# A planned attention and feed-forward kernel: VectorE chains in the planner, z in contiguous rows, other idle matmuls, a new search of priorities

## The chip, the cores and the metric

One core of a Trainium2 chip. The metric is the device time of one execution in microseconds. In a profile, PE is TensorE's matmuls and PEld its weight loads, DVE is VectorE, ACT is ScalarE, POOL is GpSimd, and SP issues the transfers.

## What is computed

```python
# per batch (8) and head (8), 576 positions, head size 64, 128 features
h   = x_scaled @ omega.T - sum(x_scaled**2) / 2
phi = exp(h - max(h)) / sqrt(128)              # for q and for k
kv  = phi_k.T @ v;  z = sum over positions of phi_k
attn = (phi_q @ kv) / (phi_q @ z + 1e-6)
# then over 4608 tokens of 512 values (heads side by side)
out = softplus(attn @ w_in) @ w_out            # 512 -> 2048 -> 512
```

All arrays are float32. The two layers are done in split form: a rounded part and a rest of both operands, three matmuls of the rounded type for one product.

## The kernel before

**Staging.** Attention is cut in sixteen quads, `Quad(n)`: one batch and four heads each. A quad's 576 positions are five tiles (`NU`), four of 128 positions and one of 64. For each tile of k or q: a load; `squares` and `norms` (sum of squares); for batches 2 to 7 `rounded` and `rest` (the operand split, L497 and L501); `project` on TensorE (L390 in batches 0 and 1, L508 later); `aside` and `join`, which add the two halves of the split projection (L511, L515); `maxima`, `bias`, `exponent` (L518, L525, L526, L530). Key tiles go on to `outer` in `plan_sums` (L589, L591): kv accumulates over tiles 0 to 2 in one bank, is put aside by `part`, and over tiles 3 and 4 in another; then `z` and `whole` add the two. z goes out to memory and comes back to all partitions (L610, L614) as `zb`. Query tiles go on to `den` (L712, four products with accumulation), `invert` (L717), `divide` (L721), `blocks` (a transpose, L744), out and in again by transfers (L757, L767), and to `num` (L834), whose result is split in `xh` and `xl` (L841, L845), the ring of 1024 tokens that layer 1 reads. Batch 0 takes a shorter way: kv in one bank, z spread by a matmul (L669), features turned by TensorE (L728).

**Feed-forward.** Tokens come in four blocks of 256 and seven of 512; each block has 16 steps, one for each 128 of the 2048 inner values. A step is layer 1 (twelve matmuls, L884 to L886, into one of two `h` banks), three activations on ScalarE (L890, L893, L896), `plus` on VectorE (L899, which frees the h bank), `high` and `low` (L903, L907: the split `gh`, `gl`), and layer 2 (three matmuls for each 128 tokens, L913 to L915).

**What sets the order.** Each of these is a `Work` with a cost on one or two engines, a due time, what it comes after, and the buffers that it takes and gives. `in_order` builds one list greedily: of all works that may start, the one that starts first, and of those that could start within PATIENCE of it on the same engine, the one due first. With two engines given (`squares`, `rest`, `divide`, `high`, `low` and others) it takes the one that ends sooner. `LAG` is the time between engines, LATE a margin on some works, and `port` keeps works of VectorE marked so apart from GpSimd's. Instructions are issued in this order, engine by engine, and each engine keeps it. `with_fill` puts idle matmuls, 512 columns each, where the plan has TensorE waiting in its first 70 us. The PSUM banks are two `at` (attention), two `h` and four `acc`; `ph` tiles have six buffers, and a query tile takes two of them (`phs` for the features, `rest` for the products) from `project` on.

Of the kernel before, what the change touches and what calls it, by code (L numbers as in the profile page):

```python
# [41 lines left out]
LEAN = {"DVE": 0.81, "POOL": 0.50, "ACT": 0.19}  # L42
SPREAD = ((0, 24.76), (18, 70.75))
# [6 lines left out]
def blocks_of(n_tokens):  # L50
# [10 lines left out]
    ("POOL", "DVE"): 0.075, ("POOL", "PE"): 0.05, ("ACT", "ACT"): 0.13, ("POOL", "POOL"): 0.1,  # L61
}


class Work:

    def __init__(
        self, on, due, emit, after=(), take=(), give=(), spare={}, behind=None, port=False, late=0.0, wire=None
    ):
        self.on, self.due, self.emit, self.port = on, due, emit, port  # L70
# [3 lines left out]
        self.wire, self.done = wire, None  # L74

# [5 lines left out]
def in_order(works, room, ahead, margin):  # L81
# [35 lines left out]
    while len(out) < len(works):  # L117
# [11 lines left out]
        for n, (_, box, key) in zip(got, w.take):  # L129
# [23 lines left out]
def with_fill(out, held, banks, until, emit):  # L153

    last, all_ = None, []
    for i, w in enumerate(out):
        if w.engine == "PE":
            t = w.end - w.on["PE"] * (2 if w.end < SLOW + 1 else 1)
            n = int((t - last - FILL) / 0.2268) if last is not None and t < until else 0
            names = [  # L160
                b for b in banks if all(x1 <= last and g < i or x0 >= t and f >= i for x0, x1, f, g in held.get(b, []))
            ] if n > 0 else []
            if names:
                all_.append((emit, names[0], n))
# [6 lines left out]
def favor_softplus_kernel(ctx, tc, q0, k0, qx, qy, kx, ky, vv, om, wi, wo, out):  # L171
# [89 lines left out]
    def plan_weights(nm, fc, due):  # L261
# [34 lines left out]
        def low_part(e):  # L296
# [5 lines left out]
            "SP", dma(0.65, 1.22, 1.7), due + 0.01, load, spare={} if last else {"w": 2},  # L302
# [5 lines left out]
        a = do(("ACT", "DVE"), (aw, dw2), due, low_bits, after=[l], port=True)  # L308
        b = do("ACT", aw, due, rebias, after=[l])
        c = do("DVE", dw, due, joined, after=[a, b], port=True)  # L310
        d = do(
            ("ACT", "DVE"), (aw, dw), due, high_part, after=[c] + (in_w if last else []), take=[("w", box, "w")], port=True,
# [17 lines left out]

    def phs(b, kind, n):
        return [("ph", b, (k, i)) for i in range(n) for k in (["phs", "rest"] if kind == "q" else ["phs"])]

    def plan_unit(q, kind, us, due, early):
# [83 lines left out]
        def exponent(j):  # L418
# [12 lines left out]
            "SP", read(size), due - 6.92, load, behind=prev.get("load"),  # L431
# [3 lines left out]
        if kind == "k" and not early:  # L435
            for i in range(len(us)):
                ldv.append(do(
                    "SP", dma(0.7, 1.0, 0.7), due + 3.31, lambda i=i: load_v(i), behind=ld, take=[("v", b, ("vs", i))]
                ))
        s = do(("POOL", "ACT"), (pool(w), act(w)), due, squares, after=[ld])  # L440
        r, sm = None, [("sm", b, "sms")]
        if not cols:
            r = do("DVE", dve(w), due + 1.34, norms, after=[s], behind=prev.get("norms"), take=sm)
# [3 lines left out]
            "PE", 0.29 + (0.44 if cols else 0.224) * nt, due + 0.86, project, after=[ld] + ([s] if cols else []),  # L447
            behind=(prev.get("project"), q.zc if kind == "q" and not early else None),
            take=[(kind_, b, ("ppb", 0)), (kind_, b, ("ppb", 1))] + (sm if cols else []) + ([] if early else phs(b, kind, len(us))),
# [16 lines left out]
        for i in range(len(us)):  # L466
            plan_queries(q, us[i], due - 0.00 * i, b, es, f"{nm}_{i}", i, i == len(us) - 1)

    def plan_split(q, kind, u, due):
# [40 lines left out]
        def aside(t):  # L510
            nc.scalar.copy(b["ph"][:, 2 * t : 2 * t + 2], b["pp"][t][:, :, 1])  # L511
# [16 lines left out]
        def exponent(t):  # L528
# [604 lines left out]
```

## Time and profile before

| | |
|---|---|
| three runs | 1073.42, 1076.78, 1080.35 us, median 1076.78 |
| the profiled execution | 1077.06 us, span 1075.3 us |
| mean granted clock of TensorE | 0.972 |
| largest groups on TensorE | layer 1 at L884 254.2 us, L885 249.2, L886 249.2; layer 2 at L913 230.0, L914 226.0, L915 225.3 |
| projections L508 for k and q | 38.4 and 36.6 us |
| kv at L589 | 41.0 and 14.3 us |
| idle matmuls | 8 of `idle` 3.7 us, 17 of `ident` 4.8 us |

The largest groups on TensorE overlap, since matmuls are pipelined; how closely they follow is read from the starts of single instructions. A row of stretches gives busy time by engine in a range; the clock in it is what TensorE was granted, 1.00 being full.

### The profile page before, as it was taken

To read this page: it belongs to the slowest core of one execution; us is meant where nothing else is said; L and a number is where in the kernel's file an instruction comes from. 1 tells how busy PE (TensorE), PEld (TensorE's weight loads), DVE (VectorE), ACT (ScalarE), POOL (GpSimd) and SP (SyncE) were. 2 spreads that over 40 slices of the span, in tenths; PEclk is the share of its full clock that TensorE was granted. 3 is DMA by queue.
4 is the path that set the end of the run, shared out by engine and by line. 5 is a ranking of instruction groups with operands and counts; after the bars stand their busy time and mean duration, and the time that the engine had idled before them with its cause. 6 is when DMAs were issued, how large, how long until landed. Compare 5 with 4: busy or idle time off the path is not lost.

```text
span 1075.3 us, 17753 instructions
## 1 busy us (share of the span) xinstructions
PE 1034.8 (96%) x5585; PEld 857.5 (80%) x5585; DVE 806.5 (75%) x2342; ACT 746.2 (69%) x1904; POOL 223.1 (21%) x218
## 2 busy tenths in 40 slices
PE   8889999999999999999999999999999999999997
PEld 7777788889887877778777787788778887888886
DVE  7889968888889898989878998888898923223222
ACT  6899967787778777767777676777667644445443
POOL 2032222133324221232232222252201200000000
PEclk7779999999999999999999999999999999999999
DMA  9843226545445454545354535553464302001001
GB/s 345 338 138 99 79 76 176 147 122 138 138 128 158 113 134 122 165 112 142 103 142 140 141 89 142 156 155 99 114 166 117 79 5 79 1 1 40 1 1 39
DMA packets 117902, 125.81 MB, mean 117 GB/s; under 512 B 17840, under 2 KB 92720, under 8 KB 117808
## 3 DMA queue, kind: packets, MB, share of 16 engines
q1 hardware_dynamic: 117808, 124.68, 40.7%
q8 instruction: 44, 0.72, 0.3%
q14 instruction: 50, 0.41, 0.1%
HBM read 98.66 MB, written 25.98 MB: 116 GB/s over the span
## 4 chain that ended last, share of the span: by engine, by line
PE 58%; DVE 26%; ACT 7%; issue 4%; DMA 4%; POOL 0%; SPq 0%; DVEq 0%; ACTq 0%; POOLq 0%
PE h L884 8%; PE h L886 8%; PE h L885 8%; PE acc L913 8%; PE acc L914 7%; PE acc L915 7%; DVE restq L712 5%; PE kv_True L589 3%; DVE u L899 2%; DMA xq<-qy 2%; DVE phk L515 2%; PE xp L834 2%; DVE smk L518 2%; DVE phq L721 2%; DVE phq L515 1%
## 5 line engine op out<-in xcount | busy, mean ns | idle before, releaser
L884 PE MATMUL h<-xh,wi 128*128 128x512 f32 (+1 forms) x704 | 254.2, 361 | 10.7 <-DVE u L899 8.9
L885 PE MATMUL h<-xl,wi 128*128 128x512 f32 (+1 forms) x704 | 249.2, 354 | 0.0
L886 PE MATMUL h<-xh,wi 128*128 128x512 f32 (+1 forms) x704 | 249.2, 354 | 0.0
L913 PE MATMUL acc<-wo,gh 128*128 128x512 f32 x576 | 230.0, 399 | 1.3 <-ACT o L949 1.3
L914 PE MATMUL acc<-wo,gh 128*128 128x512 f32 x576 | 226.0, 392 | 0.0
L915 PE MATMUL acc<-wo,gl 128*128 128x512 f32 x576 | 225.3, 391 | 0.0
L899 DVE SCALAR_TENSOR_TENSOR u<-h,u 128x512 f32<-128x512 f32 (+1 forms) x176 | 102.7, 586 | 132.1 <-ACT u L896 131.3
L884 PEld LDWEIGHTS h<-xh,wi 128*128 128x128 f32 x704 | 134.7, 191 | 36.9 <-DVE u L899 14.6
L890 ACT ACTIVATE u<-h 128x512 f32<-128x512 f32 (+1 forms) x176 | 90.9, 519 | 104.4 <-PE h L886 101.6
L886 PEld LDWEIGHTS h<-xh,wi 128*128 128x128 f32 x704 | 134.7, 191 | 18.3
L885 PEld LDWEIGHTS h<-xl,wi 128*128 128x128 f32 x704 | 134.7, 191 | 17.0
L903 ACT CAST gh<-u 128x512 fp32r<-128x512 f32 (+1 forms) x162 | 87.3, 541 | 73.5 <-PE acc L915 25.2
L907 POOL TENSOR_TENSOR gl<-u,gh 128x256 fp32r<-128x256 f32 (+1 forms) x80 | 86.1, 1078 | 248.7 <-ACT gh L903 237.6
L913 PEld LDWEIGHTS acc<-wo,gh 128*128 128x128 f32 x576 | 108.7, 189 | 26.3 <-issue 5.8
L915 PEld LDWEIGHTS acc<-wo,gl 128*128 128x128 f32 x576 | 108.5, 188 | 23.7
L914 PEld LDWEIGHTS acc<-wo,gh 128*128 128x128 f32 x576 | 108.9, 189 | 17.5
L712 DVE CUSTOM_DVE_ANT_0 restq<-phq,zb 128x128 f32<-128x128 f32 x280 | 113.0, 449 | 8.0 <-ACT phq L530 5.6
L896 ACT ACTIVATE u<-u 128x512 f32<-128x512 f32 (+1 forms) x176 | 97.7, 558 | 3.6
L893 ACT ACTIVATE u<-u 128x512 f32<-128x512 f32 (+1 forms) x176 | 97.7, 558 | 3.2
L501 POOL TENSOR_TENSOR tq<-xq,tq 64x512 fp32r<-64x512 f32 (+1 forms) x47 | 56.2, 1195 | 181.0 <-ACT tq L497 131.7
L530 ACT ACTIVATE phk<-phk,smk 128x128 f32<-128x128 f32 x216 | 70.3, 392 | 29.5 <-DVE smk L526 29.4
L907 DVE TENSOR_TENSOR gl<-u,gh 128x512 fp32r<-128x512 f32 (+1 forms) x96 | 61.3, 639 | 36.6 <-ACT gh L903 33.5
(126 smaller groups left out, 1542.1 us busy)
## 6 DMA issues: line engine op xcount, KB each, us to landing
xk<-ky SPq DMA_DIRECT2D x48, 384.0 KB, 3.5
xq<-qy SPq DMA_DIRECT2D x48, 384.0 KB, 3.3
qdq<-restq SPq DMA_DIRECT2D x56, 256.0 KB, 2.4
out<-o SPq DMA_DIRECT2D x36, 256.0 KB, 2.3
vk<-vv SPq DMA_DIRECT2D x70, 130.0 KB, 3.3
rawi<-wi SPq DMA_DIRECT2D x16, 512.0 KB, 7.2
rawo<-wo SPq DMA_DIRECT2D x16, 512.0 KB, 6.0
q<-qdq SPq DMA_DIRECT2D x64, 128.0 KB, 3.6
```

The source lines that it names most:

```text
L712: nc.vector.tensor_tensor_reduce(jk[r, c], ph[r, c], q.zb[r, h], 1.0, 1e-6, ALU.mult, ALU.add, dn[r, 0, c : c + 1])
L884: nc.tensor.matmul(b["h"], wh, xh[:, cc, t], start=cc == 0, stop=False)
L885: nc.tensor.matmul(b["h"], wh, xl[:, cc, t], start=False, stop=False)
L886: nc.tensor.matmul(b["h"], wl, xh[:, cc, t], start=False, stop=cc == NCC - 1)
L890: nc.scalar.activation(b["u"], b["h"], AF.Abs)
L893: nc.scalar.activation(b["u"], b["u"], AF.Exp, scale=-1.0)
L896: nc.scalar.activation(b["u"], b["u"], AF.Ln, bias=1.0)
L899: nc.vector.scalar_tensor_tensor(b["u"], b["h"], 0.0, b["u"], ALU.max, ALU.add)
L907: (nc.vector if e == "DVE" else nc.gpsimd).tensor_tensor(b["gl"], b["u"], b["gh"].bitcast(F32), ALU.subtract)
L913: nc.tensor.matmul(acc[tt], gh, w2[fc][:, 0], start=fc == 0, stop=False)
L914: nc.tensor.matmul(acc[tt], gh, w2[fc][:, 1], start=False, stop=False)
L915: nc.tensor.matmul(acc[tt], gl, w2[fc][:, 0], start=False, stop=fc == NFC - 1)
```

## The change

- **Planner.** `lag` between two dependent works on VectorE is 0.11 us instead of 0. A work has `soon` (it may start that much before one of its inputs is done), `steps` (stored, not used) and `heat` (columns that it streams); a taken buffer may be needed later than the start (a fourth entry in `take`). Costs of several works are set anew: `den` 0.87 for 1.27, a kv tile 0.836 for 0.89; `blocks` is marked as using the shared port.
- **Buffers.** `ph` is no longer taken at `project` but at `aside` or the first `exponent`, and `rest` at `den`.
- **kv.** One work for each key tile instead of one for all; the first may start before the last tiles are done.
- **z.** In memory [4, 128] instead of [128, 4], so that `zb` lies with the features side by side.
- **Idle matmuls.** The first eight become four each of 512, 256, 128 and 64 columns. Later ones go wherever the plan has a gap that holds one and a free bank, while fewer than 2.95 x 8192 columns were streamed in the last 3.41 us; the old rule now leaves 5.58 us of a gap (before 0.3).
- **Numbers.** All due times, LATE, PATIENCE, LEAN, SPREAD, AHEAD are searched anew.

The diff, cut to its core:

```diff
-AHEAD = 52.88
+AHEAD = 213.44
-LATE = {"num": 1.83, "turn": 3.02, "project": 0.72, "blocks": 0.00, "out": 0.00, "in": 0.07, "store": 0.10, "outer": 0.52}
+LATE = {"num": 1.25, "turn": 5.44, "project": 0.85, "blocks": 0.00, "out": 0.27, "in": 2.55, "store": 0.24, "outer": 0.27}
-SLOW = 6.63
-FILL = 0.3
-PATIENCE = {"PE": 0.00, "DVE": 0.02, "ACT": 0.00, "POOL": 0.02, "SP": 0.19}
+SLOW = 7.59
+FILL = 5.58
+UNTIL = 93.76
+HEAT = 2.95
+EXTRA = 0.00
+WINDOW = 3.4133
+PATIENCE = {"PE": 0.00, "DVE": 0.01, "ACT": 0.00, "POOL": 1.23, "SP": 1.02}
...
+    ("DVE", "DVE"): 0.11,
...
-            data = max([x.done + lag(x.engine, e) for x in w.after], default=0.0)
-            space = max([free[n][0] + lag(free[n][1], e) for n in got], default=0.0)
+            data = max([x.done + lag(x.engine, e) - w.soon.get(x, 0) for x in w.after], default=0.0)
+            space = max([free[n][0] + lag(free[n][1], e) - sum(k[3:]) for n, k in zip(got, w.take)], default=0.0)
...
-            n = int((t - last - FILL) / 0.2268) if last is not None and t < until else 0
...
+                n = int((t - last - FILL) / 0.2268) if t < UNTIL else 0
+                cool = HEAT * 8192 - sum(h for s, h in hot if s > t - WINDOW)
+                n = max(n, min(int(np.ceil(cool / 512)), int((t - last) / 0.2268 + EXTRA)))
...
-            take=[(kind_, b, ("ppb", 0)), (kind_, b, ("ppb", 1))] + (sm if cols else []) + ([] if early else phs(b, kind, len(us))),
+            take=[(kind_, b, ("ppb", 0)), (kind_, b, ("ppb", 1), 0.1 * nt)] + (sm if cols else []), heat=512 * nt,
...
-            q.zd = dram.tile([P, 4], F32, name=f"zd{q.nm}", tag="zd", bufs=2)
-            nc.sync.dma_start(q.zd, q.z)
+            q.zd = dram.tile([4, P], F32, name=f"zd{q.nm}", tag="zd", bufs=2)
+            nc.sync.dma_start(q.zd.rearrange("c m -> m c"), q.z)
...
-            "PE", 0.03 + sum(0.89 if u < 4 else 0.45 for _, _, u in keys), due + 0.10, outer, after=deps,
+    for k, (b, i, u) in enumerate(keys):
+        m = do(
+            "PE", 0.836 if u < 4 else 0.418, due + 0.62, lambda k=k: outer(k), after=[m] if k else [x for x, _ in deps],
+            soon={} if k else dict(deps), take=[] if k else [("at" if q.b > 1 else "more", y, "bank")],
...
-            "DVE", 1.27, due - 0.54, den, after=es + [q.zc], take=[("dn", b, "dns")],
+            "DVE", 0.87, due - 2.57, den, after=es + [q.zc], steps=4, soon={es[1]: 0.43} if q.b > 1 and u < 4 else {},
...
-        fill("at.0", 8, idle)
+        for i in range(4):
+            fill("at.0", 4, idle[:, : P if i < 3 else D], max(1, 4 >> i))
```

How the rows stand, at three places. First, TensorE at the start (`fill` are idle matmuls, `ppk_1_1` the projection of the second key tile of quad 1, `kv_0` quad 0's kv). Before, and then in the change:

```order
L390 MATMUL ppk_1_1_0_178<-omf,xk_1_1_110 128x128
L390 MATMUL ppk_1_1_1_179<-omf,xk_1_1_110 128x128
L390 MATMUL ppk_0_2_0_194<-omf,xk_0_2_112 128x128
L390 MATMUL ppk_0_2_1_195<-omf,xk_0_2_112 128x128
L390 MATMUL ppk_0_2_0_194<-omf,xk_0_2_112 128x128
L390 MATMUL ppk_0_2_1_195<-omf,xk_0_2_112 128x128
L645 MATMUL kv_0_220<-xk_0_0_104 128x65 x4
L645 MATMUL kv_0_220<-xk_0_1_108 128x65 x4
```

```order
L400 MATMUL ppk_1_1_0_198<-omf,xk_1_1_125 128x128
L400 MATMUL ppk_1_1_1_199<-omf,xk_1_1_125 128x128
L1043 MATMUL fill<-ident 128x512 x3
L400 MATMUL ppk_0_2_0_226<-omf,xk_0_2_127 128x128
L400 MATMUL ppk_0_2_1_227<-omf,xk_0_2_127 128x128
L400 MATMUL ppk_0_2_0_226<-omf,xk_0_2_127 128x128
L400 MATMUL ppk_0_2_1_227<-omf,xk_0_2_127 128x128
L662 MATMUL kv_0_242<-xk_0_0_117 128x65 x4
L1043 MATMUL fill<-ident 128x512 x2
```

Three idle matmuls now stand ahead of a projection and two behind the first kv; from the first projection to the turning of the first query tile there are 25 of 512 columns, where before there were five, and in the whole kernel 33 behind the initial ones instead of 17.

Second, GpSimd in the last batch (`tq_0_0` is the rest of the first query tile of that batch, `gl` a step's rest, `phq` a division). Before, and then in the change:

```order
L501 TENSOR_TENSOR tq_1_4_9326<-xq_1_4_9263,tq_1_4_9326 64x256
L907 TENSOR_TENSOR gl_11_9364<-u_11_9274,gh_11_9330 128x512
L501 TENSOR_TENSOR tk_1_0_9384<-xk_1_0_9311,tk_1_0_9384 64x512
L501 TENSOR_TENSOR tq_0_0_9442<-xq_0_0_9390,tq_0_0_9442 64x512
L721 TENSOR_TENSOR phq_1_4_9370<-phq_1_4_9370,dnq_1_4_9434 128x256
L501 TENSOR_TENSOR tk_1_1_9503<-xk_1_1_9424,tk_1_1_9503 64x512
L501 TENSOR_TENSOR tq_0_1_9557<-xq_0_1_9474,tq_0_1_9557 64x512
L907 TENSOR_TENSOR gl_15_9662<-u_15_9594,gh_15_9654 128x512
```

```order
L512 TENSOR_TENSOR tk_0_4_9269<-xk_0_4_9161,tk_0_4_9269 64x256
L925 TENSOR_TENSOR gl_9_9285<-u_9_9232,gh_9_9274 128x512
L738 TENSOR_TENSOR phq_1_3_9260<-phq_1_3_9260,dnq_1_3_9321 128x512
L738 TENSOR_TENSOR phq_1_4_9391<-phq_1_4_9391,dnq_1_4_9431 128x256
L925 TENSOR_TENSOR gl_14_9640<-u_14_9590,gh_14_9634 128x512
```

`tk_1_0`, `tq_0_0`, `tk_1_1` and `tq_0_1` are no longer on GpSimd; they stand on VectorE. Over the whole kernel GpSimd has 12 `gl` of 512 columns instead of 39, 6 whole `tq` instead of 36, 11 `tk` instead of 20, 2 weight parts instead of 9, but 30 whole divisions instead of 17 and 14 half ones instead of 4. Of the roundings ScalarE has 91 whole ones instead of 57, and VectorE 5 instead of 39; of the `high` casts of 512 columns ScalarE has 110 instead of 101.

Third, kv on TensorE (`vk_1_0`, `vk_1_1`, `vk_1_2` are the v of the first three key tiles of a quad). Before, and then in the change:

```order
L915 MATMUL acc_1_2680<-wo_1376,gl_10_3179 128x512
L589 MATMUL kv_1_2_True<-vk_1_0_2811,phk_1_0_2827 128x65 x4
L589 MATMUL kv_1_2_True<-vk_1_1_2824,phk_1_1_2986 128x65 x4
L589 MATMUL kv_1_2_True<-vk_1_2_2984,phk_1_2_3118 128x65 x4
L884 MATMUL h_14_3287<-xh,wi_1449 128x256
```

```order
L933 MATMUL acc_1_2790<-wo_1446,gl_9_3204 128x512
L606 MATMUL kv_1_2_True<-vk_1_0_2687,phk_1_0_2842 128x65 x4
L606 MATMUL kv_1_2_True<-vk_1_1_2849,phk_1_1_3036 128x65 x4
L606 MATMUL kv_1_2_True<-vk_1_2_3008,phk_1_2_3172 128x65 x4
L902 MATMUL h_13_3288<-xh,wi_1428 128x256
```

The three tiles follow each other in both. From batch 1 on there are 28 such runs of key tiles before and 29 in the change, so only one is parted.

More of the change, by code (lines that the diff above doesn't have):

```diff
@@ L315, in plan_weights @@
             in_w.append(d)
-        return do(("DVE", "POOL"), (dw, pw), due, low_part, after=[d], give=[(box, "raw")], port=True)
+        return do(("DVE", "POOL"), (dw, pw), due - 6.73, low_part, after=[d], give=[(box, "raw")], port=True)
     class Quad:
@@ L615, in in_z @@
-            q.zb = t.rearrange("p m c -> p c m")
+            q.zb = at.tile([P, 4, M], F32, name=f"zb{q.nm}", tag=q.slots["zb"], bufs=1)
+            nc.sync.dma_start(
+                q.zb.rearrange("p c m -> p (c m)"), q.zd.rearrange("c m -> (c m)").unsqueeze(0).broadcast_to([P, 4 * M])
+            )
         old = quads[q.n - 3].nums if q.n >= 3 else []
-        m = do(
-            "PE", 0.03 + sum(0.89 if u < 4 else 0.45 for _, _, u in keys), due + 0.10, outer, after=deps,
-            take=[("at" if q.b > 1 else "more", y, "bank")],
-            give=[(b, (k, i)) for b, i, _ in keys for k in ("phs", "vs")],
-            late=LATE["outer"] if q.b > 1 else 0, behind=() if first else tuple(old),
-        )
+        m = None
@@ L624, in plan_sums @@
+        for k, (b, i, u) in enumerate(keys):
+            m = do(
+                "PE", 0.836 if u < 4 else 0.418, due + 0.62, lambda k=k: outer(k), after=[m] if k else [x for x, _ in deps],
+                soon={} if k else dict(deps), take=[] if k else [("at" if q.b > 1 else "more", y, "bank")],
+                give=[(b, ("phs", i)), (b, ("vs", i))], heat=1040,
+                late=LATE["outer"] if q.b > 1 and not k else 0, behind=None if k or first else tuple(old),
+            )
         if first:
-            q.part = do("ACT", 0.29, due - 0.33, part, after=[m] + ([quads[q.n - 1].kvl] if q.n > 2 else []), give=[(y, "bank")])
+            q.part = do("ACT", 0.29, due - 25.64, part, after=[m] + ([quads[q.n - 1].kvl] if q.n > 2 else []), give=[(y, "bank")])
@@ L805, in plan_queries @@
         h = do(
-            ("ACT", "DVE"), (act(n * M, PSUM), dve(n * M)), due + 3.71, turned, after=[t], give=[(b, "tpb")],
+            ("ACT", "DVE"), (act(n * M, PSUM), dve(n * M)), due + 19.16, turned, after=[t], give=[(b, "tpb")],
         )
@@ L847, in plan_x @@
         a = do(
-            "PE", 0.26 + 0.00334 * w, due - 8.94, num, after=q.turned + [q.kvl],
-            take=[(any_, y, ("bank", p)) for p in range(2)], give=[(qt, k) for k in (["tag"] if not q.b else [("tag", i) for i in range(nq)])],
+            "PE", 0.16 + 0.00334 * w, due + 2.89, num, after=q.turned + [q.kvl], heat=8 * w,
+            take=[(any_, y, ("bank", p), (0.08 + 0.00167 * w) * p) for p in range(2)], give=[(qt, k) for k in (["tag"] if not q.b else [("tag", i) for i in range(nq)])],
             behind=tuple(old_reads(q.b, o, w)),
@@ L952, in store @@
                 nc.sync.dma_start(out[t0 + tt * P : t0 + (tt + 1) * P, :], o["t"])
-            a = do("DVE", 0.34, due + 1.55, left, after=[ends[tt]], take=[("t2", o, "s")])
-            r = do("ACT", 0.27, due - 1.98, right, after=[a], give=[(box, ("acc", i, tt))])
-            do("SP", dma(0.25, 0.8, 1.05), due + 8.00, store, after=[a, r], give=[(o, "s")], late=LATE["store"])
+            a = do("DVE", 0.34, due - 9.45, left, after=[ends[tt]], take=[("t2", o, "s")])
+            r = do("ACT", 0.27, due - 18.81, right, after=[a], give=[(box, ("acc", i, tt))])
+            do("SP", dma(0.25, 0.8, 1.05), due - 20.96, store, after=[a, r], give=[(o, "s")], late=LATE["store"])
     assert NQ == 2
```

202 lines of the change are left out of this document (105 added, 97 removed).

## Prediction

> **What bounds the kernel now.** I read the page first, then the stretches, then what TensorE waits for, then single instructions.
>
> The head of the page, and the shares of the chain that ended last:
>
> ```profile
> span 1075.3 us, 17753 instructions
> PE 1034.8 (96%) x5585; PEld 857.5 (80%) x5585; DVE 806.5 (75%) x2342; ACT 746.2 (69%) x1904; POOL 223.1 (21%) x218
> ...
> PE 58%; DVE 26%; ACT 7%; issue 4%; DMA 4%; POOL 0%; SPq 0%; DVEq 0%; ACTq 0%; POOLq 0%
> ```
>
> TensorE is the bound, and VectorE stands on the chain for a quarter of it. The profiled execution took 1077.06 us, 0.03% over the median of the three runs (1076.78), so 1.8 us lie around its span; I subtract from 1077.06. Three stretches (after the range: length, then PE, PEld, DVE, ACT and POOL busy, clock, DMA share, GB/s):
>
> ```profile
> 0.00:80.00 80.00, 69.20 (x410) 57.78 (x411) 63.20 (x264) 64.07 (x168) 17.44 (x27) 0.74 0.74 276
> 80.00:860.00 780.00, 755.96 (x4235) 627.88 (x4234) 684.30 (x1987) 584.24 (x1572) 205.70 (x192) 0.99 0.47 127
> 860.00:1075.30 215.30, 209.66 (x944) 171.81 (x942) 58.97 (x92) 97.85 (x166) 0.00 (x0) 1.00 0.07 21
> ```
>
> The last stretch is the feed-forward alone and has nothing to give: it is idle for 5.6 us in all, most of it behind the last matmul. The middle has 24.0 us of idle TensorE, with VectorE busy 88% of it (684.30 of 780). The start runs at 0.74 of the clock. The granted clock falls to half in seven stretches; two long and one short of them:
>
> ```profile
> 11.80:35.70 23.90, 23.90 (x127) 22.29 (x126) 18.07 (x69) 17.34 (x51) 4.41 (x8) 0.50 1.03 391
> 49.30:66.40 17.10, 14.16 (x61) 10.82 (x62) 15.99 (x69) 14.32 (x33) 2.88 (x3) 0.50 0.49 157
> ...
> 769.50:772.90 3.40, 3.40 (x9) 2.65 (x9) 3.19 (x7) 2.87 (x9) 0.78 (x1) 0.50 0.62 152
> ```
>
> The other four (at 134.7, 407.7, 465.7 and 520.4 us) are as short as the last. What TensorE and its weight loads wait for (us in total, times, longest):
>
> ```profile
> PEld h L884 <- DVE u L899: 14.6, 18, 2.7
> PEld kv_True L589 <- DVE phq L515: 6.7, 8, 1.5
> PEld ppq L508 <- POOL tq L501: 5.8, 4, 2.8
> ```
>
> Layer 1 waits for VectorE's `plus` to free an h bank, kv waits for a `join` to free a bank, and a query projection waits for GpSimd. One such wait in full, on TensorE and then on GpSimd (start, length, engine, line, what):
>
> ```profile
> 768.74 0.74 PE L508 MATMUL ppq<-oms,tq 128*128 128x256 f32 x4 [2.37 <-POOL tq L501]
> ...
> 770.39 0.63 PE L884 MATMUL h<-xh,wi 128*128 128x512 f32 x1
> 770.82 0.63 PE L885 MATMUL h<-xl,wi 128*128 128x512 f32 x1
> ...
> 773.42 0.39 PE L886 MATMUL h<-xh,wi 128*128 128x512 f32 x1
> 773.65 0.39 PE L913 MATMUL acc<-wo,gh 128*128 128x512 f32 x1
> ```
>
> ```profile
> 767.42 1.26 POOL L501 TENSOR_TENSOR tq<-xq,tq 64x512 fp32r<-64x512 f32 x1 [6.46 <-ACT tq L497]
> ```
>
> TensorE stands 2.37 us for a 1.26 us subtraction on GpSimd, and right behind it comes a half-clock stretch in which a 512-column matmul starts 0.43 us after the one before it, against 0.23 us at full clock. So a wait is paid twice: 2.37 us, and then half of 3.40 us.
>
> **z contiguous.** Before, the four values of a feature lie side by side, so the products at L712 step over `zb` by 16 bytes. The tiles of batch 0 read a contiguous `zb` (copied from PSUM); all others read the strided one:
>
> ```profile
> 58.60 0.29 DVE L712 CUSTOM_DVE_ANT_0 xq<-xq,zb 128x128 f32<-128x128 f32 x1
> ...
> 58.82 0.28 DVE L712 CUSTOM_DVE_ANT_0 xq<-xq,zb 128x128 f32<-128x128 f32 x1
> ```
>
> ```profile
> 568.15 0.38 DVE L712 CUSTOM_DVE_ANT_0 restq<-phq,zb 128x128 f32<-128x128 f32 x1
> ...
> 568.47 0.38 DVE L712 CUSTOM_DVE_ANT_0 restq<-phq,zb 128x128 f32<-128x128 f32 x1
> ```
>
> ```profile
> L712 DVE CUSTOM_DVE_ANT_0 restq<-phq,zb x280: 369/386/1507, 131.5 to 855.0; 128x128 f32<-128x128 f32 x112, 64x128 f32<-64x128 f32 x28
> ```
>
> From start to start 0.32 us strided, 0.22 us contiguous: 0.10 us for each of 280, **28 us less on VectorE**, all of it in the middle. The price is paid by the write of z, which becomes 512 runs of 4 bytes instead of 128 of 16:
>
> ```profile
> zd<-z SPq DMA_DIRECT2D x14, 2.0 KB, 1.9
> ...
> zb<-zd SPq DMA_DIRECT2D x14, 256.0 KB, 4.3
> ```
>
> Bounds for one: unchanged (1.9 us), or four times it (7.6). Two of the fourteen places, the read of `zb` on SP and the first product on VectorE:
>
> ```profile
> 222.95 0.33 SPq L614 DMA_DIRECT2D zb<-zd  x1
> ```
>
> ```profile
> 226.78 0.39 DVE L712 CUSTOM_DVE_ANT_0 restq<-phq,zb 128x128 f32<-128x128 f32 x1
> ```
>
> ```profile
> 542.57 0.33 SPq L614 DMA_DIRECT2D zb<-zd  x1
> ```
>
> ```profile
> 554.57 0.94 DVE L712 CUSTOM_DVE_ANT_0 restq<-phq,zb 128x128 f32<-128x128 f32 x1
> ```
>
> The first has no room, the second 12.0 - 4.3 = 7.7 us. Behind the waiting read on SP stand the loads of the next tiles and the features' DMAs; in the order of the change other DMAs go between write and read in ten of the fourteen places (before: in nine). A write 5.7 us later would at worst hold the first product for 14 x 5.7 = 80 us; with some 7 us of room at most places I take 0. The Trainium skill's page "DMA: Bandwidth & Descriptors" (Specifications) says that a transfer under 512 B is done as a read-modify-write; by that rule the dearer end is the likelier. No run here shows either end yet.
>
> **Planner, shared port, new priorities.** The order shows who takes what. The rows that price it:
>
> ```profile
> L712 DVE CUSTOM_DVE_ANT_0 restq<-phq,zb 128x128 f32<-128x128 f32 x224 | 89.5, 456 | 6.4 <-ACT phq L530 5.6 <-ACT phq L427 0.3
> ...
> L907 DVE TENSOR_TENSOR gl<-u,gh 128x512 fp32r<-128x512 f32 x73 | 50.5, 691 | 32.7 <-ACT gh L903 29.9 <-PE h L886 0.7
> ...
> L721 DVE TENSOR_TENSOR phq<-phq,dnq 128x512 f32<-128x512 f32 x39 | 33.6, 861 | 1.0
> ...
> L497 DVE CAST tk<-xk 128x512 fp32r<-128x512 f32 x24 | 10.1, 422 | 5.5 <-PE ppq L508 3.2 <-issue 1.1 <-POOL xk L489 0.9
> ...
> L501 DVE TENSOR_TENSOR tq<-xq,tq 64x512 fp32r<-64x512 f32 x12 | 8.3, 690 | 0.4
> ```
>
> ```profile
> L907 POOL TENSOR_TENSOR gl<-u,gh 128x512 fp32r<-128x512 f32 x39 | 52.6, 1348 | 141.1 <-ACT gh L903 132.5 <-issue 4.5 <-DVE gh L903 3.0
> L501 POOL TENSOR_TENSOR tq<-xq,tq 64x512 fp32r<-64x512 f32 x36 | 47.8, 1327 | 136.6 <-ACT tq L497 95.4 <-DVE tq L497 20.6 <-DMA q<-qdq 7.0
> ...
> L721 POOL TENSOR_TENSOR phq<-phq,dnq 128x512 f32<-128x512 f32 x17 | 18.2, 1072 | 11.1 <-DVE dnq L717 10.9
> ```
>
> ```profile
> L497 ACT CAST tk<-xk 128x512 fp32r<-128x512 f32 x24 | 15.0, 623 | 0.5 <-DMA xk<-ky 0.5
> ```
>
> From GpSimd to VectorE: 27 `gl` of 512 columns (27 x 0.691 = 18.7 us on VectorE, 36.4 off GpSimd), 30 `tq` differences (20.7 and 39.8), 9 `tk` (6.2 and 11.9), 7 weight parts (about 4.8 and 9.4). From VectorE to GpSimd: 13 divisions (9.0 at an undisturbed 0.69, 13.9 on GpSimd) and 10 half ones (about 4 and 6). From VectorE to ScalarE: 34 roundings (34 x 0.422 = 14.3, 21.2 on ScalarE) and 9 `gh` (3.8 and 5.6). VectorE gains about 19 us of work, ScalarE 27, and GpSimd loses 78 of its 223, a third.
>
> GpSimd's third matters for the port. While GpSimd works, some of VectorE's instructions stand: the strided products have a median of 386 ns and a maximum of 1507; the divisions have a mean of 861 where the same form of `gl` has 691, 39 x 0.17 = 6.6 us. For the 224 whole products the mean of their group (456) is 70 ns over the median, 15.7 us. A third of these 22 us gone is 7 us. So VectorE's load moves by -28 + 19 - 7 = **-16 us**, 2.3% of 684.
>
> What this is worth on TensorE: VectorE's idle time in the middle grows from 96 to 112 us, and if waits shrink as that grows, the 21.3 us of the first two wait rows (14.6 + 6.7) become 18.3: **-3**. What a better order does to the remaining 18.3 lies between nothing and all of it; the plan now counts 0.11 us between dependent VectorE instructions and a `den` of 0.87 us instead of 1.27, and takes the `ph` buffers later, so I take half: **-9**. It could be worth less than nothing: the margin LATE for `outer` falls from 0.52 to 0.27 and for `num` from 1.83 to 1.25, which puts TensorE's in-order work closer to its data; I bound that by +9. Queued behind such a matmul is all of layer 1, and ScalarE waits for that.
>
> The 5.8 us behind GpSimd: 30 of 36 whole `tq` differences leave it, and the one of the example is among them: 5.8 x 30/36, **-5** (between 0 and -5.8).
>
> **kv one work per tile.** The order keeps the tiles of a run next to each other in all but one of 28 runs, so nothing moves on TensorE: 0. The buffers of the first tiles come free one or two tiles earlier on paper; the bound is the 6.7 us of the kv row, counted above already.
>
> **Idle matmuls.** The five short stretches of half clock cost 5 x 3.40 / 2 = 8.5 us, and the one shown comes right behind a wait. With 17 of the 27 us of the named waits gone about three of the five go: **-5** (between 0 and -8.5); only 8 of the new idle matmuls lie past the early part, so they do not do it themselves. In the early part 25 stand between the first projections and kv. If they hold the clock up, the 23.90 us of work of 11.8 to 35.7 would take 12, but VectorE has 18.07 us of work there and the transfers run at 391 GB/s with a share of 1.03, so at most 5.4 us come free; in 49.3 to 66.4 VectorE's 15.99 leaves 1.1. Bounds 0 and -6.5, **-4** taken, as the clock may rise late in it. The initial eight become sixteen shorter ones, with 3840 columns for 4096: 0.
>
> **Sum.** -3 - 9 - 5 - 5 - 4 = -26: 1077.06 - 26 = **1051 us**.
>
> **Rivals.** *Nearly all waits go.* All 21.3 and 5.8, the dips' 8.5 and 6.5 of the start are 42 us: 1035; with the small waits that the rows don't name a few less, 1030. For it: the tail shows full-rate TensorE when nothing disturbs it. Against: VectorE is still at 86%.
>
> *No relief.* The 19 us moved onto VectorE and 27 onto ScalarE lengthen the chain that layer 1 waits for (ScalarE's three activations, then `plus`), and the 14.6 us row stays. Then only the start and a wait or two give: 1077 - 5 = 1072. For it: ScalarE, not only VectorE, feeds `plus`. Against: its 584 of 780 leave room.
>
> *The idle matmuls stand in the way* (slower). In 11.8 to 35.7 TensorE is busy for 23.90 of 23.90 us and yet at half clock: being busy did not raise it. If 25 matmuls of 512 columns more don't either, each costs 0.43 us on an engine without a gap there, 10.8 us, and with the +9 of thinner margins: 1077 + 20 = 1097. It decides from the point where the gaps that the plan sees (TensorE at full speed after 7.59 us) are not on the chip. The rule cannot hold back: it asks for 2.95 x 8192 = 24166 columns in 3.41 us, and a matmul every 0.23 us gives 7600, so every planned gap is filled. The Trainium skill's page "TensorE: Matmul & The Clock Gate" (Part 1) says that about 3.4 us of sustained work release the full clock; by that rule alone the stretch would have been fast from about 15 us on. The trace disagrees: seven such windows stayed at 0.50. So what counts must be more than busy, which is why I hold the dense idle matmuls for likelier to help than not.
>
> **How the numbers follow.** Forecast (1037 to 1066) 0.60; nearly all waits go 0.12; no relief 0.17; idle matmuls in the way 0.11. Over 1% either way is about what a measurement of this kernel tells from no change: faster 0.72, within 1% 0.17, slower 0.11. The range 1030 to 1075 holds the first three but for their ends. The forecast's own range is 1037 to 1066.
>
> **What would show it.** Right: products at L712's place start 0.21 to 0.22 us apart; GpSimd near 145 us, VectorE near 790, ScalarE near 773; at most two or three short half-clock stretches past 100 us; no wait of `ppq` for GpSimd over 1 us; the half-clock stretch before 36 us shorter. Wrong: TensorE idle for 24 us or more from 80 to 860; clock 0.50 from 12 to 36 with fills in it; VectorE waiting for the landing of `zb`.

## The result and the profile after

The changed kernel takes 1132.23 us (median of 4 runs, 1125.63 to 1133.14) and the kernel before 1075.1 beside it: 1.0514 times as long, 95% interval 1.0453 to 1.0576. The forecast was 1051, 0.976 times, with a range to 1075. It is slower by 57 us where 26 us less were expected. The profiled execution of the change took 1131.58 us. One execution of all that follow is left out of its ratio: of the ten of the write that is called "64 apart" in a table below, one took 2007.92 us (the median in the table is that of all ten).

The page of the changed kernel: span, busy time by engine, and the clock in 40 slices.

```profile
span 1129.8 us, 17905 instructions
PE 1044.1 (92%) x5609; PEld 867.4 (77%) x5609; DVE 752.5 (67%) x2345; ACT 762.1 (67%) x1946; POOL 147.9 (13%) x173
...
PEclk9899898999998989899989999989989899999999
```

GpSimd (147.9) and ScalarE (762.1) are near the 145 and 773 forecast, and VectorE (752.5) is 37 us below the 790. The work has moved as planned, the engines have less of it, and the kernel is slower all the same: all engines stand more. The products, at their new line:

```profile
L729 DVE CUSTOM_DVE_ANT_0 restq<-phq,zb x280: 259/287/1372, 134.6 to 903.3; 128x128 f32<-128x128 f32 x112, 64x128 f32<-64x128 f32 x28
```

The median is 287 ns against 386: the 0.10 us of each product are there. Three stretches of the changed kernel (length, then PE, PEld, DVE, ACT and POOL busy, clock, DMA share, GB/s):

```profile
15.90:50.10 34.20, 31.32 (x251) 25.11 (x248) 27.28 (x130) 30.96 (x88) 2.84 (x4) 1.00 1.01 382
80.00:860.00 780.00, 720.16 (x3995) 604.11 (x3996) 594.42 (x1849) 565.83 (x1530) 133.45 (x150) 0.96 0.48 120
860.00:915.00 55.00, 49.03 (x219) 40.54 (x218) 37.21 (x130) 31.94 (x76) 6.34 (x7) 0.94 0.42 78
```

The start runs at full clock, so the new idle matmuls do not stand in the way. The middle, which now reaches to 915 us, has 780 - 720.16 + 55 - 49.03 = 65.8 us of idle TensorE against 24.0, and a clock of 0.96 and 0.94. Read in rows of 0.8 us, the profile has thirteen half-clock stretches past 100 us, of 3.4 or 6.8 us each, 75 us in all, against five of 3.40 us before, 17 in all. What TensorE waits for (us in total, times, longest):

```profile
PE ppq L518 <- DVE phk L527: 20.1, 7, 4.3
PE ppk L518 <- DVE tk L512: 10.9, 2, 5.8
...
PE ppk L518 <- POOL tk L512: 7.0, 1, 7.0
...
PE h L902 <- DVE u L917: 4.6, 3, 4.1
```

The row of layer 1 has shrunk from 14.6 to 4.6, as was meant. In its place stand few and long waits of the projections, 3 to 7 us each. The engines that they name are not the cause; that is read from the transfers. The waits of SP's queue, first in the changed kernel and then in the kernel before:

```profile
SPq L628 <- DMA zd<-z: 93.0, 13, 9.8
```

```profile
SPq L614 <- DMA zd<-z: 17.0, 10, 2.9
```

And the landing of the two z transfers in the changed kernel (KB each, median us from issue to landing):

```profile
zb<-zd SPq DMA_DIRECT2D x14, 256.0 KB, 5.2
zd<-z SPq DMA_DIRECT2D x14, 2.0 KB, 9.9
```

The write of z lands in 9.9 us where it took 1.9: 5.2 times as long for the same 2 KB, above the dearer bound of 7.6. One of the fourteen places in full (start, length, engine, line, what, and idle time before it):

```profile
554.89 0.38 SPq L624 DMA_DIRECT2D zd<-z  x1
...
556.19 0.35 SPq L489 DMA_DIRECT2D xk<-ky  x1
...
564.92 0.33 SPq L628 DMA_DIRECT2D zb<-zd  x1
...
568.90 0.42 ACT L498 ACTIVATE xk<-xk 128x256 f32<-128x256 f32 x1 [7.80 <-DMA xk<-ky]
...
570.23 1.28 POOL L512 TENSOR_TENSOR tk<-xk,tk 64x512 fp32r<-64x512 f32 x1 [10.01 <-ACT tk L508]
...
571.57 1.22 PE L518 MATMUL ppk<-oms,tk 128*128 128x256 f32 x4 [7.05 <-POOL tk L512]
```

A row of waits would blame GpSimd for the 7.05 us. Read backward it is another story: GpSimd had been idle for 10.01 us, ScalarE for 7.80, and both, GpSimd by way of ScalarE, for the load of `xk`, issued at 556.19 and ahead of the wait on SP, yet in the tile only at 568.9. The load was not queued late; it was slow. Four microseconds into the wait the clock falls as well:

```profile
568.90:575.70 6.80, 4.13 (x12) 3.46 (x13) 4.80 (x19) 6.77 (x19) 2.29 (x3) 0.50 0.58 171
```

Behind thirteen of the fourteen writes such a stretch begins, 12 to 21 us after the write was issued; behind the one at 622.19 there is none. Stretches of the changed kernel around the place shown, and one behind another write, tell what the transfers did:

```profile
549.00:555.00 6.00, 6.00 (x35) 5.17 (x34) 5.49 (x17) 5.03 (x14) 1.77 (x2) 1.00 0.48 140
557.00:567.00 10.00, 7.52 (x35) 5.94 (x34) 5.04 (x18) 2.46 (x6) 0.61 (x1) 1.00 0.53 23
390.30:398.40 8.10, 8.10 (x42) 5.99 (x41) 5.11 (x12) 5.12 (x12) 0.61 (x1) 1.00 0.00 0
```

The last two columns are the reading. In the second stretch the transfer engines are as busy as in the first (0.53 against 0.48) and move a sixth of the bytes (23 GB/s against 140); two loads of this place had been issued at 556. The third lies behind the write of 388.31, which lands by 398.49, and there no load stands behind it: the share is 0.00. So it is not the write that counts as busy, but the loads behind it, which wait in the engines and carry almost nothing until it has landed.

### The profile page after: what moved, and what is told of

It is laid out like the page before. It is cut to its first block, busy times and chain, and to the rows that moved or that the text cites. A ratio compares the mean times of both kernels' runs of the same rounds, so it can differ in the third digit from the quotient of the medians.

```text
span 1129.8 us, 17905 instructions
## 1 busy us (share of the span) xinstructions
PE 1044.1 (92%) x5609; PEld 867.4 (77%) x5609; DVE 752.5 (67%) x2345; ACT 762.1 (67%) x1946; POOL 147.9 (13%) x173
## 5 line engine op out<-in xcount | busy, mean ns | idle before, releaser
L931 PE MATMUL acc<-wo,gh 128*128 128x512 f32 x576 | 233.7, 406 | 0.0
L932 PE MATMUL acc<-wo,gh 128*128 128x512 f32 x576 | 229.9, 399 | 0.0
L933 PE MATMUL acc<-wo,gl 128*128 128x512 f32 x576 | 229.2, 398 | 0.0
L902 PEld LDWEIGHTS h<-xh,wi 128*128 128x128 f32 x704 | 136.8, 194 | 28.9 <-DVE u L917 5.7
L904 PEld LDWEIGHTS h<-xh,wi 128*128 128x128 f32 x704 | 135.9, 193 | 18.8
L921 ACT CAST gh<-u 128x512 fp32r<-128x512 f32 (+1 forms) x172 | 93.2, 542 | 58.4 <-PE acc L933 27.6
L933 PEld LDWEIGHTS acc<-wo,gl 128*128 128x128 f32 x576 | 110.9, 193 | 24.6
L931 PEld LDWEIGHTS acc<-wo,gh 128*128 128x128 f32 x576 | 110.9, 193 | 24.0 <-issue 4.5
L932 PEld LDWEIGHTS acc<-wo,gh 128*128 128x128 f32 x576 | 111.1, 193 | 17.8
L925 DVE TENSOR_TENSOR gl<-u,gh 128x512 fp32r<-128x512 f32 (+1 forms) x120 | 77.6, 647 | 52.4 <-ACT gh L921 51.5
L729 DVE CUSTOM_DVE_ANT_0 restq<-phq,zb 128x128 f32<-128x128 f32 x280 | 73.5, 294 | 18.9 <-DMA zb<-zd 11.2
L925 POOL TENSOR_TENSOR gl<-u,gh 128x256 fp32r<-128x256 f32 (+1 forms) x56 | 50.3, 900 | 182.2 <-ACT gh L921 158.0
L738 POOL TENSOR_TENSOR phq<-phq,dnq 128x512 f32<-128x512 f32 (+1 forms) x44 | 40.7, 925 | 254.0 <-DVE dnq L734 116.6
```

What stands on the lines that cost most here:

```text
L902: nc.tensor.matmul(b["h"], wh, xh[:, cc, t], start=cc == 0, stop=False)
L904: nc.tensor.matmul(b["h"], wl, xh[:, cc, t], start=False, stop=cc == NCC - 1)
L921: (nc.scalar.copy if e == "ACT" else nc.vector.tensor_copy)(b["gh"], b["u"])
L925: (nc.vector if e == "DVE" else nc.gpsimd).tensor_tensor(b["gl"], b["u"], b["gh"].bitcast(F32), ALU.subtract)
L931: nc.tensor.matmul(acc[tt], gh, w2[fc][:, 0], start=fc == 0, stop=False)
L932: nc.tensor.matmul(acc[tt], gh, w2[fc][:, 1], start=False, stop=False)
```

## The experiments

**Theory Z:** the four-byte write costs it all, because it holds the transfer engines, so that loads behind it come late, TensorE waits once per quad, and each such wait is followed by a half-clock stretch. **Rivals:** the planner's thinner margins and new order did it; or only the products wait, for `zb`. The first four kernels ran on one chip beside the kernel before (1073.48 us).

### The change with the old z

```diff
-            q.zd = dram.tile([4, P], F32, name=f"zd{q.nm}", tag="zd", bufs=2)
-            nc.sync.dma_start(q.zd.rearrange("c m -> m c"), q.z)
+            q.zd = dram.tile([P, 4], F32, name=f"zd{q.nm}", tag="zd", bufs=2)
+            nc.sync.dma_start(q.zd, q.z)
...
-            q.zb = at.tile([P, 4, M], F32, name=f"zb{q.nm}", tag=q.slots["zb"], bufs=1)
...
+            t = at.tile([P, M, 4], F32, name=f"zb{q.nm}", tag=q.slots["zb"], bufs=1)
+            nc.sync.dma_start(t.rearrange("p m c -> p (m c)"), q.zd.rearrange("m c -> (m c)").unsqueeze(0).broadcast_to([P, 4 * M]))
+            q.zb = t.rearrange("p m c -> p c m")
```

> The changed kernel with z alone put back: written as 128 runs of 16 bytes, read by the strided view, the order of every engine otherwise that of the change. Theory Z (the write of z in 512 runs of 4 bytes holds the transfer queues some 9 us once per quad, and that is the whole loss): 1045 to 1070 us, no projection waits over 2 us on TensorE. Theory O (the newly searched order with thinner margins is at fault, z only rides along): 1115 to 1135 us with the same waits of L518.

Measured: 1046.53 us (1045.49 to 1047.41), ratio 0.9748, interval 0.9700 to 0.9796. Its middle, and its two z transfers:

```profile
80.00:840.00 760.00, 751.07 (x4255) 630.69 (x4254) 659.89 (x1982) 602.35 (x1614) 141.22 (x157) 1.00 0.47 129
```

```profile
zb<-zd SPq DMA_DIRECT2D x14, 256.0 KB, 4.0
zd<-z SPq DMA_DIRECT2D x14, 2.0 KB, 2.5
```

TensorE is idle for 8.9 us of its middle and the clock is 1.00. Everything in the change but z is worth 27 us of gain; z's lines alone turn that into the loss. The rival of the thinner margins falls. 1132.23 - 1046.53 = 85.7 us go to z's lines (the two were measured apart; by the two ratios it is 82), of which 65.8 - 8.9 = 57 are idle TensorE. The other 29 fit the 75 us of half clock, which can cost up to half their length; with the old z no such stretch is left past 100 us.

### The kernel before with the new z alone

The same edit the other way round, on the kernel before:

```diff
-            q.zd = dram.tile([P, 4], F32, name=f"zd{q.nm}", tag="zd", bufs=2)
-            nc.sync.dma_start(q.zd, q.z)
+            q.zd = dram.tile([4, P], F32, name=f"zd{q.nm}", tag="zd", bufs=2)
+            nc.sync.dma_start(q.zd.rearrange("c m -> m c"), q.z)
...
```

The read of `zb` becomes the contiguous one with it.

> The kernel before with the new z alone: written as 512 runs of 4 bytes, read contiguously; order unchanged. Theory Z: the landing of the write goes from 1.9 to about 10 us and the time to 1095 to 1125 us, though VectorE saves 28 us. Theory O: 1060 to 1080 us.

Measured: 1181.84 us (1175.19 to 1183.74), ratio 1.1001, interval 1.0946 to 1.1056. The loss is larger than expected, 108 us. The write lands late here too:

```profile
zd<-z SPq DMA_DIRECT2D x14, 2.0 KB, 10.5
```

So the price hangs on the write and not on the new order; the new order even bears it better (86 us against 108).

### An unread write of four-byte runs

The kernel before keeps its z, and writes it a second time, behind the first, in the new form. Nothing reads that copy.

```diff
             nc.sync.dma_start(q.zd, q.z)
+            zx = dram.tile([4, P], F32, name=f"zx{q.nm}", tag="zx", bufs=2)
+            nc.sync.dma_start(zx.rearrange("c m -> m c"), q.z)
```

> The kernel before with one more write of z for each quad, in 512 runs of 4 bytes to a place that nothing reads, behind the old write on SP's queue. If the small runs hold the transfer engines themselves, the loads behind them land late though nothing waits for this write: 1085 to 1115 us. If only SP's wait for the landing costs: 1072 to 1080 us.

Measured: 1175.55 us (1174.62 to 1182.08), ratio 1.0966, interval 1.0913 to 1.1020.

```profile
zd<-z SPq DMA_DIRECT2D x14, 2.0 KB, 4.1
zx<-z SPq DMA_DIRECT2D x14, 2.0 KB, 12.0
```

102 us for a write that nothing reads, far above the 1085 to 1115 us expected. What waits for z in this kernel, first SP for the old write and then the products for `zb`:

```profile
SPq L616 <- DMA zd<-z: 19.5, 10, 6.2
DVE restq L714 <- DMA zb<-zd: 8.6, 3, 3.4
```

SP waited 17.0 us for the write in the kernel before, and for the new one its queue names two waits, 9.4 us in all. So nearly all of this loss comes without SP's waiting, and the 93.0 us that it waits in the changed kernel are not needed to explain one. The second rival falls too: 8.6 us of waiting for `zb` are small beside 102. What is lost comes through the other transfers (the old write beside the new takes 4.1 us instead of 1.9). All transfers of the kernel are issued by SP on one queue, so no run here tells whether the write holds the engines for every queue or only what stands in its own. The Trainium skill's page "DMA: Bandwidth & Descriptors" (Back-pressure in remote DMA) says of another kind of transfer that stalled writes stall the other queues of the engine that sends them too; no run here has a second queue to show it.

### z turned on VectorE

Contiguous in memory too, but the short runs are avoided: VectorE transposes z in blocks of 32 by 32, and four transfers write runs of 128 bytes. This replaces the change's write; the read of `zb` stays contiguous.

```diff
+    zs = const.tile([P, 32], F32, name="zs")
+    zt = const.tile([P, 32], F32, name="zt")
+    nc.vector.memset(zs, 0.0)
...
+            nc.vector.transpose(zt, zs)
...
-            nc.sync.dma_start(q.zd.rearrange("c m -> m c"), q.z)
+            for i in range(4):
+                nc.sync.dma_start(q.zd[:, 32 * i : 32 * i + 32], zt[32 * i : 32 * i + 4, :])
```

z itself now lies in the first four columns of `zs`, and an unused tile of 80 columns makes room for the two.

> The changed kernel with z turned on VectorE first (a 32x32 block transpose of z in a tile of 32 columns), then written as sixteen runs of 128 bytes by four transfers; the read stays contiguous. Theory Z: landing about 2 us, 1035 to 1060 us, at or a little under the first experiment. Theory O: 1115 to 1135 us.

Measured: 1041.83 us (1039.8 to 1042.7), ratio 0.9705, interval 0.9664 to 0.9746. This is the lowest median of the study. Its middle, and the one wait for GpSimd that is left:

```profile
80.00:840.00 760.00, 758.42 (x4305) 638.73 (x4304) 641.76 (x2004) 608.21 (x1627) 140.21 (x157) 1.00 0.46 130
```

```profile
PE acc L937 <- POOL gl L929: 0.2, 1, 0.2
```

TensorE is idle for 1.6 us out of 760, against 24.0 out of 780 before. The price on VectorE (busy us, mean ns, idle before):

```profile
L619 DVE STREAM_TRANSPOSE zt<-zs 128x32 f32<-128x32 f32 x14 | 3.0, 212 | 0.5
```

Fourteen times 0.21 us, for products that are as short as in the change.

### z turned in the kernel before

The kernel before with `zs` and `zt` as above and the contiguous read of the change:

```diff
+            nc.vector.transpose(zt, zs)
...
-            q.zd = dram.tile([P, 4], F32, name=f"zd{q.nm}", tag="zd", bufs=2)
-            nc.sync.dma_start(q.zd, q.z)
+            q.zd = dram.tile([4, P], F32, name=f"zd{q.nm}", tag="zd", bufs=2)
+            for i in range(4):
+                nc.sync.dma_start(q.zd[:, 32 * i : 32 * i + 32], zt[32 * i : 32 * i + 4, :])
```

> The kernel before with nothing changed but z: turned on VectorE, written in runs of 128 bytes and read contiguously. If the shorter products are worth what the prediction gave them (3 us by the wait rows, and some of the half-clock dips), 1066 to 1073 us, ratio 0.990 to 0.997. If most of what the change with z turned gained over the kernel before (31 us) comes from the shorter products, 1045 to 1055 us. If the products are hidden behind TensorE, 1073 to 1078 us. In all three VectorE is busy for some 28 us less than before's 806, and the write of z lands in 2 to 3 us.

Measured: 1064.03 us (1058.67 to 1065.14), ratio 0.990, interval 0.9851 to 0.9949; the middle:

```profile
80.00:860.00 780.00, 767.60 (x4338) 638.41 (x4337) 668.82 (x2027) 596.67 (x1599) 206.89 (x195) 1.00 0.45 128
```

The shorter products bring 8 us by the change in medians (against 1072.47 for the kernel before beside it), 2 us more than the first of the expected ranges holds: the idle time of the middle falls from 24.0 to 12.4 us and the half-clock stretches in it are gone. So the larger part of the gain of 31 us is the planner's and the order's (27 with the old z); the two parts taken alone come to 35, a little more than both together.

### Why the write is slow: count or neighbours

Runs of four bytes are short, 512 of them are many, and they lie side by side in memory, neighbours from different partitions. Five unread writes in the kernel before tell these apart. The edit in each is the destination:

```diff
-            zx = dram.tile([4, P], F32, name=f"zx{q.nm}", tag="zx", bufs=2)
-            nc.sync.dma_start(zx.rearrange("c m -> m c"), q.z)
+            zx = dram.tile([4, P, 128], F32, name=f"zx{q.nm}", tag="zx", bufs=2)
+            nc.sync.dma_start(zx[:, :, 0].rearrange("c m -> m c"), q.z)
```

This puts the runs 512 bytes apart; with 16 or 4 in the place of 128 they are 64 or 16 bytes apart; `dram.tile([P, 4])` with `q.z` writes 128 runs of 16 bytes, and `dram.tile([P, 1])` with `q.z[:, :1]` 128 runs of 4.

> The kernel before with an additional write of z that nothing reads, in 512 runs of 4 bytes as in the experiment with the unread write (1175.6 us), but each run 512 bytes from the next, so that no two of them are neighbours. If it is the number of small runs that holds the transfer engines, the same as there: 1160 to 1185 us. If it is that neighbouring runs fall together, the hold goes: 1075 to 1100 us and a landing below 4 us.

> The kernel before with an additional write of z that nothing reads, in 128 runs of 16 bytes as the kernel's own. If a fourth of the runs holds the engines a fourth as long, some 25 us over the kernel before: 1095 to 1105 us. If the hold starts only where the runs are shorter or more numerous than this, 1073 to 1083 us. An additional DMA instruction alone (0.33 us on the queue, 14 times) is worth nothing here.

> The unread write of z once more, in 512 runs of 4 bytes, each 64 bytes from the next (before: 4 bytes apart, 1175.6 us; 512 bytes apart, 1087.3 us). If runs disturb each other only inside the same 64 bytes, as with 512 bytes: 1083 to 1092 us and a landing of about 4 us. If the stretch that they must not share is longer, or the whole write has to reach over more memory, between 1100 and 1175 us and a landing of 5 to 12 us.

> The same with 16 bytes from run to run, so that 4 runs share 64 bytes where the neighbours 4 bytes apart have 16. If what counts is how many runs fall into the same 64 bytes, the hold is some 4 of 16 parts of the neighbours': landing 5 to 7 us, 1095 to 1115 us. If it is enough that any two share them, as with neighbours: above 1150 us. If the stretch is 16 bytes or less, 1083 to 1092 us.

> An unread write of the first of the four columns of z alone: 128 runs of 4 bytes, neighbours 4 bytes apart, a quarter of the unread write that brought 1175.6 us. If the neighbours' hold goes with the number of runs, a quarter of its 102 us: 1095 to 1105 us and a landing of 4 to 5 us. If the first runs to fall together already hold the engines, above 1120 us. If up to 128 small runs are free, neighbours or not (128 of 16 bytes gave 1077.5 us), 1073 to 1080 us.

| unread write | median us | ratio, interval |
|---|---|---|
| 512 runs of 4 bytes, 4 apart | 1175.55 | 1.0966, 1.0913 to 1.1020 |
| 512 runs of 4, 16 apart | 1093.27 | 1.0190, 1.0138 to 1.0243 |
| 512 runs of 4, 64 apart | 1083.50 | 1.0081, 1.0049 to 1.0114 |
| 512 runs of 4, 512 apart | 1087.32 | 1.0123, 1.0077 to 1.0169 |
| 128 runs of 4, 4 apart | 1148.47 | 1.0694, 1.0645 to 1.0743 |
| 128 runs of 16, side by side | 1077.52 | 1.0030, 1.0001 to 1.0059 |

Each ratio is against the kernel before, run beside it (medians 1073.48 us for the first row, 1072.47 for the two of 512 apart and of 16 bytes, 1073.32 for the other three). The landings, in the order of the five expectations, one row from each kernel:

```profile
zx<-z SPq DMA_DIRECT2D x14, 2.0 KB, 3.8
```

```profile
zx<-z SPq DMA_DIRECT2D x14, 2.0 KB, 2.6
```

```profile
zx<-z SPq DMA_DIRECT2D x14, 2.0 KB, 3.6
```

```profile
zx<-z SPq DMA_DIRECT2D x14, 2.0 KB, 4.4
```

```profile
zx<-z SPq DMA_DIRECT2D x14, 0.5 KB, 8.7
```

The same 512 runs of 4 bytes, moved apart, land in 3.6 to 3.8 us instead of 12.0, and of the 102 us of loss 10 to 15 are left. A quarter of the runs left side by side still lands in 8.7 us and loses 75. So it is not the count alone: it is neighbours. With 64 bytes from run to run nothing is left that 512 bytes would take away, with 16 (four runs in 64 bytes) the effect is small, 4.4 us and 20 us of loss, which lies between two of the ranges expected of it, and with 4 (sixteen runs in 64 bytes) it is the whole. Of the 128 runs a quarter of the loss was held possible, or none; what came is the third case, above 1120 us, in which the first runs to fall together already do the harm. The 128 runs of 16 bytes, of which four share 64 bytes, land in 2.6 us; they reach over the same 2 KB as the slow write, so it is not the reach alone either. Between 16 and 64 bytes nothing was tried, so where the effect ends is open. What the memory does with runs that fall together is not seen in a trace; that each waits for the one before is a guess from 8.7 us for sixteen and 4.4 for four.

### The change with z turned, without the early idle matmuls

```diff
-FILL = 5.58
+FILL = 99.0
...
-HEAT = 2.95
+HEAT = 0.00
```

All 33 idle matmuls behind the initial ones go with this, the 25 of the start among them.

> The change with z turned (1041.8 us) without the 25 idle matmuls of 512 columns that stand between the first projections and kv; the sixteen short ones ahead of them stay. The computation is the same. If they hold the clock up and it is worth what the prediction gave the start (4 us, at most 6.5), 1044 to 1049 us, with a half-clock stretch of 15 us or more ahead of 40 us. If the work of the start hangs on VectorE and the transfers whatever the clock, 1041 to 1043 us, though the clock falls. If they stand in the way, below 1040 us.

Measured: 1044.86 us (1041.59 to 1047.83), ratio 0.9731, interval 0.9683 to 0.9778. It overlaps the interval of the kernel with them (0.9664 to 0.9746), so the medians do not tell the two apart. The traces do. Stretches of the two, without the idle matmuls first:

```profile
13.50:40.80 27.30, 27.30 (x140) 24.58 (x138) 16.43 (x75) 19.70 (x61) 0.80 (x2) 0.50 1.03 389
```

```profile
13.70:47.80 34.10, 32.55 (x256) 25.88 (x256) 27.98 (x136) 31.43 (x91) 2.84 (x4) 1.00 1.03 393
```

The first is at half clock from end to end, the second at full clock. Three places of the two kernels, each time first without the idle matmuls and then with them: the first turning of a query tile (`tpq`), a later turning, and the first matmul of layer 2.

```profile
44.19 2.23 PE L749 MATMUL tpq<-ident,xq 128*128 128x128 f32 x8
40.18 0.63 PE L749 MATMUL tpq<-ident,xq 128*128 128x128 f32 x4
```

```profile
61.60 1.97 PE L749 MATMUL tpq<-ident,xq 128*128 128x128 f32 x8 [9.25 <-ACT xq L439]
56.57 1.97 PE L749 MATMUL tpq<-ident,xq 128*128 128x128 f32 x8 [9.01 <-ACT xq L439]
```

```profile
80.71 0.40 PE L935 MATMUL acc<-wo,gh 128*128 128x512 f32 x1
80.28 0.39 PE L935 MATMUL acc<-wo,gh 128*128 128x512 f32 x1
```

The idle matmuls do what they are for: the kernel with them is 4.0 us ahead at the first place and 5.0 at the second, though the transfers are at a share of 1.03 either way. At the third the lead has shrunk to 0.4. It is lost behind a wait of 9 us for ScalarE (L439), which both kernels have and which the kernel before has not (its longest wait of TensorE from 36 to 80 us is 1.6). The stretches behind that wait, again without the idle matmuls first:

```profile
61.50:68.00 6.50, 6.40 (x44) 5.41 (x46) 5.81 (x37) 5.43 (x15) 0.00 (x0) 0.76 0.00 0
56.50:68.00 11.50, 11.43 (x60) 9.36 (x61) 7.88 (x46) 7.04 (x17) 0.00 (x0) 0.50 0.27 97
```

The kernel with the idle matmuls goes on at 0.50, the other one at 0.76, which fits that the lead is lost here; no run tries that by itself. Four executions of each kernel are too few to say what is left of it in the whole.

## Why the prediction was wrong

**z contiguous, the write: the step that failed.** The prediction bounded the landing at 1.9 to 7.6 us, worked out that the dearer end could hold products for 80 us in all, and then took 0, "with some 7 us of room at most places". That term measured 82 to 86 us. Three things were wrong with it. The landing was 9.9: four times the runs gave 5.2 times the time, and the unread writes show that the number of runs was the wrong measure, since neighbours count. The room was measured at the wrong reader: it is room of the first product, for which VectorE waits only 11.2 us in all, while the loads of later tiles lose some 10 us of transfer whether or not anything waits for z (102 us for a write without a reader). And a price with a bound of 80 was left out of the range. The working named the loads behind the read on SP, but as queued behind a wait; the load at 556.19 had been issued before it. The Trainium skill's page "DMA: Bandwidth & Descriptors" (Specifications), from which the prediction took the dearer end for the likelier, pointed the right way, and it was set aside with no row against it. The rule itself does not tell 4 bytes from the 16 of before, nor 4 bytes side by side from 4 bytes apart, which the runs do.

**z contiguous, the products.** Right: 386 to 287 ns, 28 us by that sum. By the kernel before with z turned they are worth 8 us on the whole, more than the 3 of the wait rows: with the waits the half-clock stretches went as well.

**Planner, port, priorities.** Right in size, by the change with the old z. The prediction's sum without the 3 us for VectorE's load is 23; 27 came. The middle's idle time went from 24.0 to 8.9 us, 15 where 9 + 5 were predicted for waits. The wait on GpSimd's differences has gone (0.2 us is all that is left in the kernel with z turned). The margin LATE, bounded at +9, did no harm that can be seen. What VectorE loses by standing, which the prediction laid to GpSimd's work, was sized too low: a third of 22 us was to go, and nearly all went. The whole products in the changed kernel:

```profile
L729 DVE CUSTOM_DVE_ANT_0 restq<-phq,zb 128x128 f32<-128x128 f32 x224 | 56.9, 294 | 17.8 <-DMA zb<-zd 11.2 <-ACT phq L542 4.3 <-ACT phq L437 1.9
```

Their mean lies 7 ns over the median of 287 where it lay 70 over (19 with the old z), and the divisions on VectorE take 689 ns instead of 861. That is some 13 us of the 37 by which VectorE came out below the forecast; the rest was not followed up.

**Half-clock stretches.** The prediction gave three of the five, 5 us. With the old z or with z turned none is left past 100 us, which is worth up to 5 x 3.40 / 2 = 8.5 us, the prediction's bound. The changed kernel shows the other side: thirteen, and the one looked at in full begins within a wait of 7.05 us.

**Idle matmuls at the start.** The clock of the first long stretch rose as held likely, and the 4 us came, at 40 us; 0.4 of them were left at the first matmul of layer 2. The prediction looked at the two half-clock stretches of the old order alone. The new order has a wait of 9 us on ScalarE from 47.6 to 56.6, and in the kernel with z turned the clock is 0.50 from there to 68. The bound has a slip too: 23.90 - 18.07 is 5.8, not 5.4.

**kv in one work per tile.** Taken as 0 and not tried by itself.

**The rivals.** None of the three is what happened to the time. The slower one, idle matmuls in the way, falls (clock 1.00 from 15.9 to 50.1), although the time came out slower as it said. "Nearly all waits go" is what the middle does once z is out of the way (1.6 us idle), and its 1035 is missed by 7, about the 6.5 that it counted on from the start. The rival that was needed stood in the text as a bound: the write of z holds the transfers. The 26 us forecast came true, as 27, in the kernel without that edit, and there the closeness of the two numbers is in part luck: the waits and the half-clock stretches gave more than their terms, the shorter products (3 us) are not in it, and of the start's 4 little is left in the kernel with z turned.

## What to carry to other kernels

Before a layout is turned in a transfer to memory, look at what its short runs do to each other: neighbours of 4 bytes written in one transfer cost these kernels 75 to 108 us, while 512 runs of 4 bytes set 64 bytes apart, or 128 of 16 bytes, cost at most 15. Turn the tile on an engine first (0.2 us on VectorE for 128x32 here) and write long runs. When a transfer's landing time is unknown, price it by what shares the transfer engines with it, not only by who reads it, and if the bound of a step is larger than the whole gain, the range has to reach it.

## What the runs showed of the hardware that was not expected

- Loads that stand behind a small write can count as busy and carry almost nothing: share 0.53 and 23 GB/s for 10 us behind a write of 2 KB, against 0.48 and 140 GB/s ahead of it. With no load behind it the share is 0.00 while the write is under way.
- The landing of such a write goes by how close its four-byte runs lie: 12.0 us for 512 of them 4 bytes apart, 4.4 at 16 bytes, 3.6 at 64 and 3.8 at 512; 128 runs 4 bytes apart are enough for 8.7.
- TensorE busy for 27.30 of 27.30 us stays at 0.50, and the same start with some 20 matmuls of 512 columns more in it runs at 1.00. The Trainium skill's page "TensorE: Matmul & The Clock Gate" (Part 1) counts a time of sustained work and not a number of matmuls; the first stretch does not fit that, if a TensorE that the profile calls busy is sustained work.
- An end of the half clock can be spent again: 4 to 5 us won by 57 us had become 0.4 by 80, behind a wait of 9 us and a stretch at 0.50.
